# The causal mask of expert attention, moved from a TensorE matmul into the VectorE operation that takes the row maximum

## The chip, the cores and the metric

The kernel runs on one core of a Trainium2 chip, as one launch. The metric is the device time of that core in microseconds (us). A core has TensorE (PE; its weight loads are shown as PEld), VectorE (DVE), ScalarE (ACT), GpSimd (POOL) and SyncE (SP, which issues DMAs). Each works through its own queue in order and waits on semaphores for the others. SBUF and PSUM are the on-chip memories of 128 partitions; matmuls write PSUM.

## The reference

Three stages follow each other: a sparse attention of 8 heads, a mixing stage (rotation by a learned angle, token mixing, channel mixing), and an attention with four experts per batch. Only the last is touched. Cut to what matters:

```python
logits = x @ w_gate                      # x: 4 batches, 576 positions, 512 wide
# w[:, :, e]: softmax over the two largest of the 4 logits, 0 for the others
for e in range(4):
    q = x @ wq[e]; k = x @ wk[e]; v = x @ wv[e]          # 64 wide
    scores = (1 / 8) * (q @ k.transpose(0, 2, 1))         # 576 x 576
    causal = np.triu(np.ones((S, S), dtype=bool), 1)
    scores = np.where(causal, -1000000000.0, scores)
    scores = scores - scores.max(-1, keepdims=True)
    a = np.exp(scores)
    a /= a.sum(-1, keepdims=True) + 1e-09
    out += w[:, :, e:e+1] * (a @ v @ wo[e])
```

## The kernel before

The expert stage runs over 4 batches and 4 experts, and for each of these 16 pairs (function `attention`) over five tiles of queries t = 0 to 4, of 128 rows each and 64 in the last. Tile t scores against the 128(t+1) keys that causality leaves, so 128, 256, 384, 512 and 576; the last goes in two chunks of 288, since a score tile is 512 wide. That makes 80 tiles and 96 chunks. Products are made from a high and a low part of their operands.

Per chunk, PE multiplies q by the keys (line 585) and by their low part (586) into a PSUM tile `s`, of which there are three. In the last chunk of a tile a third matmul (588) adds the causal mask: the table `mask_cr`, 0 on and below the diagonal and a large negative number above it, times an identity `identr`. This matmul covers only the 128 (or 64) columns of the diagonal block. DVE then takes the negated row maximum `nm` from `s` (590; 597 joins the two chunks of tile 4). ACT computes Exp of `s` with `nm` as bias, writes the SBUF tile `p` and collects the row sum `sm` (601). Each such ACT line stands as two instructions in the trace: the Exp, and the read of the accumulator. DVE adds 1e-9 to `sm` and inverts it (605, 606), POOL scales `p` by it and by the gate (608; DVE does it for tile 0), PE transposes `p` into PSUM `tp` (611), ACT copies that to `pthi` (619), DVE makes the low part `ptlo` (620), and the matmuls of lines 563 and 567 multiply with the values. `p` has four buffers, so a tile's `p` can be written once the transposes of the tile four earlier are done.

Between the tiles stand units of other work (`fill`), released after a tile's last score matmul: the projections of the next pair and batch (`pq`, `pv`, with `q`, `k`, `klow`, `lg` made from them by ACT, DVE and POOL), and the output products `po` of the batch before. The functions give the dependencies and a rough sequence; a list scheduler then sets the order of each engine's queue from a simulated timeline. At the stage's start six POOL memsets clear halves of the low key tiles `klow` (449), then `lg` (458), whose zeros DVE overwrites in part (485).

## Time and profile before

| | us |
|---|---|
| median of 3 runs | 572.19 (572.13 to 573.19) |
| profiled execution, span | 571.5 |
| PE busy in it | 534.9 (94%) |
| DVE busy | 409.1 (72%) |
| ACT busy | 320.0 (56%) |
| POOL busy | 230.5 (40%) |

The times are of whole executions; the span is what the profiler recorded of one, and the rows are on its clock. The duration in a row is that of one instruction; where the next one of the same engine starts before it has ended, the distance from start to start is shorter than the duration. The expert stage takes the time from about 374 us to the end; some of its first projections lie before.

### The profile page before, as it was taken

The numbers are of one execution on the slowest core, as the hardware profiler recorded it, in microseconds if no ns is written. First come the engines' busy times: TensorE is split into PE (matmuls) and PEld (weight loads), VectorE is DVE, ScalarE is ACT, GpSimd is POOL, SyncE is SP. The second block draws the span as 40 slices with busy tenths as digits, with TensorE's granted clock in tenths as the row PEclk, the third lists the DMA queues.
The fourth block names the chain that finished last, engine by engine and source line by source line (L and its number), as shares of the span: only waits on it lengthen the run. The fifth ranks groups of instructions, "written<-read, shape, count | busy, mean of one in ns | idle before, by whom it ended". The sixth has DMA issues, their size and how long they took to land.

```text
span 571.5 us, 12545 instructions
## 1 busy us (share of the span) xinstructions
PE 534.9 (94%) x4536; PEld 509.9 (89%) x4536; DVE 409.1 (72%) x1211; ACT 320.0 (56%) x906; POOL 230.5 (40%) x317
## 2 busy tenths in 40 slices
PE   6859698899999999999999999898999999999987
PEld 6748598899999999999999999897989999999987
DVE  3898799757686556766356553588988898888972
ACT  5875976525435326263152450375778767857873
POOL 3453565421156111545104570354454634644451
PEclk9959889999999999999999999998999999999999
DMA  9659443333122004110100020100001101100012
GB/s 291 216 171 307 132 156 96 87 95 124 37 86 86 16 23 133 37 30 1 56 1 1 1 58 0 38 1 2 0 11 43 33 1 32 51 4 12 32 43 84
DMA packets 20390, 37.55 MB, mean 66 GB/s; under 512 B 2904, under 2 KB 10248, under 8 KB 20328
## 3 DMA queue, kind: packets, MB, share of 16 engines
q1 hardware_dynamic: 20328, 36.74, 20.4%
q8 instruction: 36, 0.59, 0.5%
q14 instruction: 26, 0.21, 0.1%
HBM read 32.01 MB, written 4.72 MB: 64 GB/s over the span
## 4 chain that ended last, share of the span: by engine, by line
PE 64%; DVE 17%; ACT 11%; DMA 3%; issue 3%; POOL 2%; SPq 0%; DVEq 0%; POOLq 0%; ACTq 0%
PE y L256 6%; PE y L257 6%; PE y L258 6%; PE s L181 3%; PE th L256 3%; PE th L258 3%; PE th L257 3%; PE tp L611 3%; DVE X L133 2%; PE g L257 2%; PE g L256 2%; PE av L234 2%; PE g L258 2%; DVE nm L590 2%; DMA k<-in_kl 2%
## 5 line engine op out<-in xcount | busy, mean ns | idle before, releaser
L256 PE MATMUL y<-wtk_hi,zhi 128*128 128x288 f32 x288 | 86.5, 301 | 0.5 <-DVE X L339 0.4
L257 PE MATMUL y<-wtk_lo,zhi 128*128 128x288 f32 x288 | 85.9, 299 | 0.0
L258 PE MATMUL y<-wtk_hi,zlo 128*128 128x288 f32 x288 | 84.7, 296 | 0.0
L324 POOL TENSOR_TENSOR zlo<-cs,zhi 128x512 fp32r<-128x512 f32 (+1 forms) x40 | 48.4, 1221 | 66.5 <-DVE zhi L321 45.5
L208 POOL TENSOR_TENSOR p<-p,sm 128x288 f32<-128x288 f32 (+2 forms) x48 | 30.6, 643 | 93.4 <-DVE sm L207 54.0
L608 POOL TENSOR_SCALAR p<-p,sm,gt 128x256 f32<-128x256 f32 (+1 forms) x64 | 45.2, 708 | 52.7 <-DVE sm L606 35.3
L601 ACT ACTIVATE p<-s,nm 128x128 f32<-128x128 f32 (+2 forms) x96 | 49.5, 518 | 14.4 <-DVE nm L590 7.9
L256 PEld LDWEIGHTS y<-wtk_hi,zhi 128*128 128x128 f32 x288 | 54.0, 188 | 1.7 <-DVE X L339 1.1
L252 POOL TENSOR_TENSOR x_lo<-X,x_hi 128x576 fp32r<-128x576 f32 x24 | 35.7, 1491 | 46.9 <-DVE x_hi L250 40.5
L257 PEld LDWEIGHTS y<-wtk_lo,zhi 128*128 128x128 f32 x288 | 54.1, 188 | 0.3
L258 PEld LDWEIGHTS y<-wtk_hi,zlo 128*128 128x128 f32 x288 | 53.9, 188 | 0.1
L256 PE MATMUL th<-wth_hi,x_hi 128*128 128x256 f32 (+1 forms) x160 | 48.4, 303 | 3.3 <-ACT X L241 2.9
L590 DVE TENSOR_REDUCE nm<-s 128x1 f32<-128x128 f32 (+2 forms) x96 | 44.3, 469 | 5.3 <-PE s L588 4.4
L258 PE MATMUL th<-wth_hi,x_lo 128*128 128x256 f32 (+1 forms) x160 | 46.2, 290 | 0.0
L181 PE MATMUL s<-k,q 128*108 128x54 f32 (+2 forms) x320 | 43.8, 282 | 2.5 <-DMA k<-in_kl 2.5
L257 PE MATMUL th<-wth_lo,x_hi 128*128 128x256 f32 (+1 forms) x160 | 46.1, 289 | 0.0
L181 PEld LDWEIGHTS s<-k,q 128*108 128x108 f32 (+1 forms) x320 | 42.0, 203 | 3.8 <-issue 2.3
L215 ACT COPY pt<-tp 96x384 f32<-96x384 f32 (+2 forms) x44 | 20.9, 477 | 36.2 <-PE tp L211 36.0
L256 PE MATMUL pq<-x_hi,wqk_hi 128*128 128x288 f32 x128 | 39.8, 311 | 1.0 <-DVE q L536 0.7
L256 PE MATMUL g<-u_hi,wch_hi 128*128 128x288 f32 x128 | 39.2, 306 | 0.0
L620 DVE TENSOR_TENSOR ptlo<-tp,pthi 128x128 fp32r<-128x128 f32 (+4 forms) x80 | 37.7, 479 | 1.1 <-ACT pthi L619 0.6
L257 PE MATMUL pq<-x_lo,wqk_hi 128*128 128x288 f32 x128 | 38.0, 297 | 0.0
(173 smaller groups left out, 1728.7 us busy)
## 6 DMA issues: line engine op xcount, KB each, us to landing
X<-in_wtk SPq DMA_DIRECT2D x18, 288.0 KB
q<-in_qs SPq DMA_DIRECT2D x8, 594.0 KB
q<-in_ql SPq DMA_DIRECT2D x8, 576.0 KB
v<-in_vl SPq DMA_DIRECT2D x24, 144.0 KB
out_t<-X SPq DMA_DIRECT2D x20, 128.0 KB
k<-in_kl SPq DMA_DIRECT2D x8, 304.0 KB
k<-in_ks SPq DMA_DIRECT2D x8, 288.0 KB
X<-in_wth SPq DMA_DIRECT2D x8, 256.0 KB
```

The lines of the kernel that those rows point to most:

```text
L181: nc.tensor.matmul(s[:rm, i * kw:i * kw + w], qt[:, j0 + i, :], kt[:, k0:k0 + w], start=False, stop=i == n - 1)
L208: nc.gpsimd.tensor_tensor(tiles(p), tiles(p), each(sm), op=ALU.mult)
L215: copy(pt[:kw, :n * rm], tp[:kw, :n * rm])
L252: eng.tensor_tensor(lo, x, f(hi), op=ALU.subtract)
L256: nc.tensor.matmul(ps, ahi, bhi, start=first, stop=False)
L257: nc.tensor.matmul(ps, ahi, blo, start=False, stop=False)
L258: nc.tensor.matmul(ps, alo, bhi, start=False, stop=last)
L324: nc.gpsimd.tensor_tensor(lo, zf, f(hi), op=ALU.subtract)
L590: nc.vector.tensor_reduce(nm[:w, t + ci:t + ci + 1], s[:w, :c1 - c0], axis=AX.X, op=ALU.max, negate=True)
L601: nc.scalar.activation(p[:w, c0:c1], scs[ci][:w, :c1 - c0], AF.Exp, bias=nm[:w, t:t + 1], scale=1.0, accum_out=acc)
L608: eng.tensor_scalar(p[:w, :kn], p[:w, :kn], sm[:w, t:t + 1], gt[:w, t, e:e + 1], op0=ALU.mult, op1=ALU.mult)
L620: nc.vector.tensor_tensor(dst(ptlo), src, f(dst(pthi)), op=ALU.subtract)
```

## The change

The mask matmul goes, and with it the tables `mask_c`, `identr` and `mask_cr`. A table `later` of 128 x 640 (bf16) takes their place: 512 columns of zeros and 128 of the diagonal mask. One DVE operation per chunk (`tensor_tensor_reduce`) adds the right stretch of it to `s`, negates, writes the result to `p`, and takes the minimum into `nm`. Exp then reads `p`, with scale −1, and writes it in place. The PSUM tile `s` is thus free after the DVE operation.

```diff
-    mask_c = new_mask("mask_c", [128, 128], const)
-    select(mask_c, [[-1, 128]], 0, 1, MASKED)
...
-    identr, mask_cr = (cw.tile([128, 128], F32R, name=name) for name in ("identr", "mask_cr"))
-    nc.vector.tensor_copy(identr, ident)
-    nc.vector.tensor_copy(mask_cr, mask_c)
+    later = cw.tile([128, 640], BF16, name="later")
+    nc.gpsimd.memset(later[:, :512], 0.0)
+    nc.gpsimd.memset(later[:, 512:], 0.0)
+    select(later[:, 512:], [[-1, 128]], 0, 1, MASKED)
...
-                nc.tensor.matmul(s[:w, :c1 - c0], q[:, ts], kl[:, c0:c1], start=False, stop=not last)
-                if last:
-                    scored = nc.tensor.matmul(s[:w, t0 - c0:t0 - c0 + w], identr[:, :w], mask_cr[:, :w],
-                                              start=False, stop=True)
-                nc.vector.tensor_reduce(nm[:w, t + ci:t + ci + 1], s[:w, :c1 - c0], axis=AX.X, op=ALU.max,
-                                        negate=True)
+                scored = nc.tensor.matmul(s[:w, :c1 - c0], q[:, ts], kl[:, c0:c1], start=False, stop=True)
+                z0 = 512 - t0 + c0 if c1 == kn else 0
+                nc.vector.tensor_tensor_reduce(p[:w, c0:c1], s[:w, :c1 - c0], later[:w, z0:z0 + c1 - c0], op0=ALU.add,
+                                               op1=ALU.min, scale=-1.0, scalar=3.0e38,
+                                               accum_out=nm[:w, t + ci:t + ci + 1])
...
-                nc.scalar.activation(p[:w, c0:c1], scs[ci][:w, :c1 - c0], AF.Exp, bias=nm[:w, t:t + 1], scale=1.0,
+                nc.scalar.activation(p[:w, c0:c1], p[:w, c0:c1], AF.Exp, bias=nm[:w, t:t + 1], scale=-1.0,
                                      accum_out=acc)
```

The queue of DVE in batch 0 where expert 3 begins and expert 2 ends, before. The names carry the expert, the tile and the chunk (`s_3_1_0`: expert 3, tile 1, first chunk), then a running number; the brackets say on which engines an instruction waits:

```order
L590 TENSOR_REDUCE nm_3_5441<-s_3_1_0_5474 128x1 [waits PE_49]
L620 TENSOR_TENSOR ptlo_2_5260<-tp_2_1_5331,pthi_2_5259 128x2x128 [waits Activation_49]
L605 TENSOR_SCALAR sm_3_5440<-sm_3_5440 128x1 [waits Activation_49]
L509 TENSOR_REDUCE mx_5317<-gt_5100 128x5 [waits DVE_49]
L620 TENSOR_TENSOR ptlo_2_5260<-tp_2_2_5346,pthi_2_5259 128x3x128 [waits Activation_49]
L536 SCALAR_TENSOR_TENSOR q_0_1_5367<-pq_0_0_1_5448,q_0_1_5367 64x288 [waits Activation_49]
L606 RECIPROCAL sm_3_5440<-sm_3_5440 128x1 [waits DVE_49]
L510 TENSOR_SCALAR mx_5317<-mx_5317 128x5 [waits DVE_49]
L605 TENSOR_SCALAR sm_3_5440<-sm_3_5440 128x1 [waits Activation_49]
L590 TENSOR_REDUCE nm_3_5441<-s_3_2_0_5508 128x1 [waits PE_49]
L540 TENSOR_TENSOR klow_0_4666<-pq_0_1_0_5479,k_0_0_5368 64x288 [waits Activation_49]
```

And now; a line called ISA is the fused operation or, with one column and no source, the read of its accumulator:

```order
L615 TENSOR_TENSOR ptlo_2_5247<-tp_2_1_5316,pthi_2_5246 128x2x128 [waits Activation_49]
L600 TENSOR_SCALAR sm_3_5422<-sm_3_5422 128x1 [waits Activation_49]
L506 TENSOR_SCALAR cnt_5287<-cnt_5287 128x20 [waits DVE_49]
L585 ISA p_3_1_5454,nm_3_5423<-s_3_1_0_5455,later 128x256 [waits PE_49,Pool_49]
L585 ISA nm_3_5423 128x1
L615 TENSOR_TENSOR ptlo_2_5247<-tp_2_2_5330,pthi_2_5246 128x3x128 [waits Activation_49]
L601 RECIPROCAL sm_3_5422<-sm_3_5422 128x1 [waits DVE_49]
L507 TENSOR_TENSOR gt_5091<-gt_5091,cnt_5287 128x20 [waits DVE_49,Activation_49]
L535 SCALAR_TENSOR_TENSOR q_0_0_5349<-pq_0_0_1_5429,q_0_0_5349 64x288 [waits Activation_49]
L603 TENSOR_SCALAR p_3_0_5424<-p_3_0_5424,sm_3_5422,gt_4676 128x128 [waits DVE_49]
L508 TENSOR_REDUCE mx_5302<-gt_5091 128x5 [waits DVE_49]
L600 TENSOR_SCALAR sm_3_5422<-sm_3_5422 128x1 [waits Activation_49]
```

The fused operation of tile 1 stands behind the low part of the older expert's tile 1 and not ahead of it, is followed by a second instruction, and waits for POOL as well as PE, since the POOL scale and the transposes of an older tile use the same buffer of `p`.

The queue of ACT at the same place, before:

```order
L601 ACTIVATE p_3_0_5442,sm_3_5440<-s_3_0_0_5443,nm_3_5441 128x128 [waits Pool_49]
L619 CAST pthi_2_5259<-tp_2_2_5346 128x3x128 [waits PE_49]
L535 ACTIVATE q_0_1_5367<-pq_0_0_1_5448 64x288 [waits DVE_49]
L601 ACTIVATE p_3_1_5473,sm_3_5440<-s_3_1_0_5474,nm_3_5441 128x256 [waits DVE_49,Pool_49]
L539 CAST k_0_0_5368<-pq_0_1_0_5479 64x288 [waits PE_49]
L572 COPY tmp_2_0_5357<-o_2_0_5352 64x256 [waits PE_49,Activation_49]
L619 CAST pthi_2_5259<-tp_2_3_5391 128x4x128 [waits PE_49]
```

And now:

```order
L596 ACTIVATE p_3_0_5424,sm_3_5422<-p_3_0_5424,nm_3_5423 128x128 [waits DVE_49]
L614 CAST pthi_2_5246<-tp_2_2_5330 128x3x128 [waits PE_49]
L505 ACTIVATE gt_5091<-lg_5088 128x20 [waits DVE_49]
L534 ACTIVATE q_0_0_5349<-pq_0_0_1_5429 64x288 [waits PE_49]
L596 ACTIVATE p_3_1_5454,sm_3_5422<-p_3_1_5454,nm_3_5423 128x256 [waits DVE_49]
L534 ACTIVATE q_0_1_5350<-pq_0_0_1_5429 64x288 [waits DVE_49]
L538 CAST k_0_0_5351<-pq_0_1_0_5459 64x288 [waits PE_49]
```

The wait for POOL has left the Exp line: it reads and writes the tile that DVE has already written.

The queue of POOL at the start of the expert stage, before:

```order
L102 TENSOR_TENSOR wvg_lo<-wvg_st_4251,wvg_hi 128x260 [waits DMAHW0_49,Activation_49]
L102 TENSOR_TENSOR wvg_lo<-wvg_st_4255,wvg_hi 128x260 [waits DMAHW1_49,Activation_49]
L449 MEMSET klow_0_4662 64x576 [waits PE_49,Pool_49]
L449 MEMSET klow_1_4663 64x576
L449 MEMSET klow_0_4664 64x576
```

And now:

```order
L100 TENSOR_TENSOR wvg_lo<-wvg_st_4250,wvg_hi 128x260 [waits DMAHW1_49,Activation_49]
L442 MEMSET later 128x512 [waits PE_49]
L443 MEMSET later 128x128
L448 MEMSET klow_0_4659 64x576 [waits Pool_49]
L448 MEMSET klow_1_4660 64x576
```

Two memsets of `later` stand ahead of the six of `klow`, behind which `lg` follows in both, and the wait for PE has passed from the first of `klow` to the first of `later`.

## Rows read from the trace of the kernel before

**Rows 1.** Engine windows of the expert stage (columns named in its first line).

```profile
core 0: us, PE busy (x) PEld busy (x) DVE busy (x) ACT busy (x) POOL busy (x), PEclk, DMA share, GB/s
...
496.00:552.00 56.00, 55.92 (x438) 53.96 (x436) 49.09 (x182) 41.10 (x129) 26.03 (x47) 1.00 0.08 28
...
sum 197.50, PE 188.66 PEld 179.01 DVE 163.78 ACT 141.43 POOL 92.57; mean PE 37.73 PEld 35.80 DVE 32.76 ACT 28.29 POOL 18.51
```

**Rows 2.** Chain of waits by line: 374 to 390, 390 to 460, 460 to 496, 496 to 552.

```profile
by line: DVE nm L590 21.8%; DVE x_lo L252 17.4%; DVE q L536 11.4%; ACT wo_hi L100 7.2%; ACT x_hi L248 7.2%; ACT p L601 6.5%; ACT k L539 4.8%; DVE ptlo L620 3.3%; issue 3.1%; DVE sm L605 3.0%; DVE klow L540 2.8%; ACT q L535 2.6%; DVE X L573 
by line: PE tp L611 10.2%; PE s L585 7.6%; PE o L567 6.9%; PE s L586 6.3%; PE pv L258 5.9%; PE o L563 5.5%; PE pv L256 5.2%; PE pv L257 5.1%; PE pq L257 4.8%; DVE nm L590 4.8%; PE pq L256 4.7%; PE pq L258 4.6%; ACT p L601 4.1%; DVE ptlo L62
by line: DVE nm L590 16.2%; DVE q L536 10.3%; ACT p L601 9.8%; DVE ptlo L620 8.8%; issue 8.2%; DVE klow L540 7.1%; DVE X L573 6.2%; DVE x_lo L252 4.4%; ACT x_hi L248 4.0%; DVE p L608 3.5%; DVE sm L606 3.4%; DVE cmp L500 2.9%; DVE sm L605 2.
by line: PE tp L611 12.5%; PE s L585 8.8%; PE pq L256 8.6%; PE o L567 8.2%; PE s L586 8.0%; PE pq L257 7.9%; PE pq L258 7.6%; PE o L563 6.6%; PE po L256 5.2%; PE po L257 4.6%; PE po L258 4.6%; PE pv L256 3.8%; PE pv L258 3.5%; PE pv L257 3.
```

**Rows 3.** Instruction groups by form: busy us, mean ns of one, then idle before.

```profile
L293 ACT ACTIVATE cs<-cs,halfpi 128x256 f32<-128x256 f32 x32 | 15.9, 497 | 0.1
...
L588 PE MATMUL s<-mask_cr,identr 128*128 128x128 f32 x64 | 15.2, 238 | 0.0
...
L590 DVE TENSOR_REDUCE nm<-s 128x1 f32<-128x512 f32 x16 | 10.9, 683 | 0.3 <-PE s L588 0.2
L620 DVE TENSOR_TENSOR ptlo<-tp,pthi 128x512 fp32r<-128x512 f32 x16 | 10.9, 681 | 0.5 <-ACT pthi L619 0.4
...
L601 ACT ACTIVATE p<-s,nm 128x256 f32<-128x256 f32 x16 | 7.6, 475 | 3.9 <-DVE nm L590 3.4 <-POOL p L608 0.2 <-DVE sm L605 0.2
...
L590 DVE TENSOR_REDUCE nm<-s 128x1 f32<-128x128 f32 x16 | 4.6, 285 | 3.0 <-PE s L588 2.9
```

**Rows 4.** Timeline of PE, 445.4 to 446.4: start us, duration us, instruction.

```profile
445.62 0.44 PE L585 MATMUL s<-k,q 128*128 128x512 f32 x1
445.90 0.39 PE L586 MATMUL s<-klow,q 128*128 128x512 f32 x1
446.13 0.22 PE L588 MATMUL s<-mask_cr,identr 128*128 128x128 f32 x1
446.19 0.29 PE L585 MATMUL s<-k,q 128*64 128x288 f32 x1
```

**Rows 5.** Timeline of DVE, 390.5 to 391.5.

```profile
390.77 0.13 DVE L605 TENSOR_SCALAR sm<-sm 128x1 f32<-128x1 f32 x1
390.83 0.47 DVE L620 TENSOR_TENSOR ptlo<-tp,pthi 128x320 fp32r<-128x320 f32 x1
```

**Rows 6.** Timeline of ACT, 427.2 to 427.5.

```profile
427.23 0.19 ACT L601 ACTIVATION_READ_ACCUMULATOR p<-s,nm 64x1 f32 x1
427.32 0.48 ACT L601 ACTIVATE p<-s,nm 64x288 f32<-64x288 f32 x1
```

**Rows 7.** What PE idled for before the first score matmul: us, times.

```profile
  ACT p L601: 2.9, 8
```

**Rows 8.** Timeline of DVE and ACT, around 379.5 and around 552.

```profile
379.27 0.45 DVE L590 TENSOR_REDUCE nm<-s 64x1 f32<-64x288 f32 x1
...
379.74 0.52 ACT L619 CAST pthi<-tp 128x128 fp32r<-128x128 f32 x2
...
551.40 0.44 DVE L590 TENSOR_REDUCE nm<-s 64x1 f32<-64x288 f32 x1
...
553.13 0.27 ACT L619 CAST pthi<-tp 128x128 fp32r<-128x128 f32 x1
```

**Rows 9.** Timelines of POOL, DVE and PE at the stage's start.

```profile
357.10 3.70 POOL L449 MEMSET klow<- 64x576 f32 x6 [14.27 <-PE g L258]
...
360.89 0.16 DVE L485 COPY lg<-pv 128x4 f32<-128x4 f32 x1 [0.80 <-POOL lg L458]
...
361.20 0.36 PE L256 MATMUL pv<-wvg_hi,x_hi 128*128 128x260 f32 x1 [0.53 <-DVE lg L485]
```

## The prediction

> **What bounds the kernel now.** The change touches the expert stage, the last 197.5 us of the span of 571.5, and a few instructions before it. I read four views, widest first. The engine windows over that stage [rows 1] show TensorE (PE) and VectorE (DVE) both near full: 189 and 164 us busy of 197.5, and in the stretch 496–552 PE is busy for 55.92 of 56.00 while DVE is busy for 49.09, which leaves DVE 12% free. So work taken from PE and given to DVE has little room. The chain of waits by line [rows 2] says who sets the pace where. In 390–460 and 496–552 only PE lines stand ahead: PE-run stretches, 126 us. In 374–390 and 460–496 the reduce that is changed leads the chain (21.8 and 16.2%), with other DVE lines behind it: DVE-run stretches, 52 us. The remaining 19.5 us (552–571.5) are the tail. So I weigh a PE saving spread evenly over the stage with 126/197.5 = 0.64 and a DVE cost with 52/197.5 = 0.26.

> Next I read the durations by form [rows 3] and then the start times on PE and DVE [rows 4, 5], because the busy time of one instruction overlaps the next on both engines: what an instruction costs is the distance from its start to the start of the next.

> **Removed: the mask matmuls.** There are 80 (16 batch-expert pairs of 5 tiles), 64 of them 128 columns wide and 16 of them 64 wide. Their rows say 238 ns each [rows 3], which would make some 18 us for the 80; that is not their price. On the timeline [rows 4] the mask matmul starts at 446.13 and the next matmul at 446.19: 0.06 us. The matmul behind it is slower as well: the first score matmul of 512 columns stands right behind a mask matmul and takes 0.28 (445.62 to 445.90), the second of equal size, not behind one, takes 0.23 (445.90 to 446.13). So 0.06 + 0.05 = 0.11 us each, 64 × 0.11 = 7.0; for the 16 narrow ones I take about half, 1.0. Together 8.0 us of PE. If the extra 0.05 stays with whatever comes next, only 64 × 0.06 and half of that for each narrow one, 16 × 0.03, go: 4.3; if the full busy time counted, 18. I take 8.0: the start times are the nearest rows. On the path: 8.0 × 0.64 = −5.1 us.

> **Changed: the row maximum.** 96 reduces of PSUM become 96 fused operations that read the same PSUM scores and a bf16 mask from SBUF and write the negated sum to SBUF beside the minimum. No row of before has this operation. The nearest is the subtraction that also reads PSUM and SBUF and writes SBUF: 681 ns at 512 columns, against 683 for the reduce [rows 3]. So the main part: 0. Lower end: below nothing is excluded, since it reads the same number of elements. Upper end: two passes per element. From 285 ns at 128 to 683 at 512 the reduce pays 1.04 ns per element [rows 3]; a partition sees 16 × (128 + 256 + 384 + 512 + 576) = 29,696 elements, so +31 us of DVE. I take 0 and keep 31 for a rival.

> **Added: an accumulator read per operation.** The program now has a second DVE instruction behind each of the 96, which writes the maximum. Nearest rows: a one-column DVE operation starts at 390.77 and the next at 390.83, 0.06 us [rows 5]; ScalarE's (ACT) own accumulator read takes 0.19 and its successor starts 0.09 after it [rows 6]. Ends: 96 × 0.06 = 5.8 and 96 × 0.19 = 18.2 us of DVE. I take 0.08, between the two start-to-start rows: 7.7 us. In DVE-run stretches 7.7 × 0.26 = +2.0. Elsewhere the PE cover hides it: in 496–552 DVE would go to 49.09 + 2.2 = 51.3 of a stretch that has shrunk to 53.7, still covered, with 4% to spare. If that cover is gone, all 7.7 count.

> **Changed: Exp reads SBUF in place.** Rows: Exp of 128x256 from PSUM 475 ns, an ACT function of the same size with a bias operand from SBUF 497 [rows 3]: +22 ns, 96 × 0.022 = 2.1 us of ACT, which is on the chain for about a tenth (4.1 to 9.8% at the Exp line [rows 2]): +0.2. [...]

> **Moved: the release of buffers.** Two things swap. (a) The three score buffers in PSUM are freed by the DVE operation and no more by Exp. PE waited 2.9 us for Exp in front of the first score matmul [rows 7]; I take −1, since some of it only changes its name. (b) The SBUF tile p (four of them) is now written by DVE about 1.1 us before Exp wrote it, and DVE must wait until the transposes of the tile four earlier are done. In order of tiles, 33 of 76 reduces began before their slot was free. The first: 379.27, while the ACT copy that follows those transposes begins only at 379.74; the last: 551.40 against 553.13 [rows 8]; the longest such lead was 3.3 us and all together make 47. What is queued behind on DVE is the low-part subtraction, the small sums and the gate work, for which ACT, POOL and PE wait. The new order puts the fused operation behind such work of older tiles (the DVE rows shown with the change), so that most of the lead is taken out by order. Ends: 0 and 6 (about an eighth of 47); I take +1.

> **Added: the table `later`.** Two POOL memsets stand before the six of `klow` and take over their wait for PE. The six take 3.70 us for 576 columns each, so 640 columns cost 3.70/6 × 640/576 = 0.7. Behind them waits the chain klow, lg, DVE's copy at 360.89 (0.80 idle), PE at 361.20 (0.53 idle) [rows 9]: all of it late by 0.7, so +0.7, less if POOL starts them earlier. The removed memset, selection and two casts of the old mask stood at the kernel's start and beside other work: 0.

> **Sum.** −5.1 + 2.0 + 0.2 − 1 + 1 + 0.7 = −2.2 us. On the profiled span of 571.5 that is 569.3; the median 572.19 lies 0.7 above that span, so the forecast is 570.0.

> **Rivals.** *No change:* the matmul behind keeps its 0.05, PE gets back 4.3 × 0.64 = 2.8, and the additions of 2.0 + 0.2 + 0.7 (a and b cancelling) eat it: 0.1 net, about 572. For it: the surplus appears on every matmul of another weight behind a narrow one. Against: the second score matmul, now ahead of it, is wide.

> *Slower: DVE becomes the bound.* The accumulator read takes its full 0.19 without overlap (18.2 us) and the fused operation holds DVE's queue for its p slot. Then DVE in 496–552 needs 49.09 + 18.2 × 56/197.5 = 54.3 plus waits, against PE's 53.7: PE's saving no longer shows. It decides from about 0.16 us per read on, or less with waits. Price: no PE gain, 18.2 × 0.26 = 4.7 in the DVE-run stretches, and up to 6 of waits, less the 1 of (a), plus 0.9: 572.2 + 5 to 10, most of it at the lower end; I set 577. For it: DVE has only 12% free and the lead of 47 us. Against: start-to-start distances of small operations on two engines are 0.06 and 0.09.

> *Much slower: half rate.* DVE gets +31 + 7.7; its 164 us become 203 for a stage of 197.5, with some waits around it: near 590. Against it: the subtraction with the same kinds of operands runs at full rate [rows 3]. [...] No run shows the operation itself.

> **Chances and range.** Forecast 46% (its own range 566 to 571), no change 19%, DVE-bound 26%, half rate 9%. From these: faster by over 0.2% (1.14 us, about what a measurement of this kernel can tell) 0.46, within 0.2% 0.19, slower 0.35. The range reaches down to 565, where PE's saving comes through with no DVE cost (−5.1 − 1 − 1), and up to 580, through most of the DVE-bound case; half rate lies outside.

> **What would show it.** Right: the accumulator read starts its successor within 0.1 us; the fused operation of 512 columns takes about 0.68; PE in 496–552 stays at 99% over a shorter stretch; the PE-run windows end some 4 to 5 us earlier in all; the first score matmul of 512 columns takes 0.23. Wrong: a fused operation near 1.1 us; DVE idle with POOL or PE as the releaser before the fused line, for more than 6 us in all; PE idle for DVE in stretches that PE ran before; a start of the stage later by more than 1 us.

## The result, and the profile after

The changed kernel takes 577.72 us (median of 4; 576.99 to 580.66) against 572.27 of the kernel before; the ratio is 1.0097, with a 95% interval of 1.0074 to 1.0119. It is slower, by about 1%. A later job (a session in which runs and the kernel before are measured together) gave 1.0100 (1.0059 to 1.0141). Over all jobs the kernel before has medians of 572.3 to 573.4, so experiments are compared by their ratios to it in the same job, not by single medians.

The windows of the expert stage, on the times of [rows 1] (the columns are those named there):

```profile
496.00:552.00 56.00, 53.48 (x408) 50.30 (x408) 47.59 (x204) 41.86 (x125) 25.07 (x44) 1.00 0.08 28
552.00:575.20 23.20, 18.68 (x113) 16.92 (x112) 7.69 (x29) 8.06 (x26) 4.64 (x8) 0.76 0.16 52
sum 201.20, PE 188.23 PEld 173.44 DVE 163.43 ACT 146.92 POOL 93.19; mean PE 37.65 PEld 34.69 DVE 32.69 ACT 29.38 POOL 18.64
```

DVE is busy no longer than before (163.43 against 163.78), though 96 instructions were added. But PE, which was full in 496–552, is now 2.5 us short of it (over the whole of 374–552 it is busy for 169.6 of 178 us, before for 173.8), and in the tail its granted clock is 0.76 on average. The forms that answer to [rows 3]:

```profile
L585 DVE CUSTOM_DVE_ANT_0 p<-s,later 128x512 f32<-128x512 f32 x16 | 11.0, 685 | 1.2 <-POOL p L603 0.6 <-POOL olo L637 0.5
...
L596 ACT ACTIVATE p<-p,nm 128x256 f32<-128x256 f32 x16 | 8.1, 509 | 0.5 <-DVE nm L585 0.2
...
L585 DVE DVE_READ_ACCUMULATOR2_ANT nm<- 128x1 f32 x64 | 5.2, 82 | 0.0
```

The fused operation is as fast as the reduce was (685 ns against 683), Exp from SBUF is 34 ns slower, and the accumulator read lasts 82 ns. What DVE's own timeline shows of that read (start, duration):

```profile
551.88 0.67 DVE L585 CUSTOM_DVE_ANT_0 p<-s,later 128x512 f32<-128x512 f32 x1
...
552.48 0.08 DVE L585 DVE_READ_ACCUMULATOR2_ANT nm<- 128x1 f32 x1
552.48 0.48 DVE L615 TENSOR_TENSOR ptlo<-tp,pthi 128x320 fp32r<-128x320 f32 x1
```

The next instruction starts with the read. From the fused operation to the next work it is 0.61 us at 512 columns (median of 16), from the reduce it was 0.60: the read is all but free.

The price is in another view: what DVE idled for in front of the fused line, and who waited for that line (us, times):

```profile
its engine sat idle before it (us, times) until:
  PE tp L606: 5.4, 10
...
  PEld s L582: 3.4, 9
  PE s L582: 0.9, 3
```

The reduce never waited for transposes (it waited 4.6 us, for scores alone). Now DVE stands still for 5.4 us until PE has transposed an older tile and so freed a buffer of p. One such place, for the last pair's tile 0, in the timeline of the changed kernel:

```profile
545.92 0.44 PE L606 MATMUL tp<-ident,p 128*128 128x128 f32 x2
...
546.30 0.19 ACT L596 ACTIVATION_READ_ACCUMULATOR p<-p,nm 64x1 f32 x1
...
546.51 0.29 DVE L585 CUSTOM_DVE_ANT_0 p<-s,later 128x128 f32<-128x128 f32 x1 [1.28 <-PE tp L606]
...
547.60 0.16 DVE L601 RECIPROCAL sm<-sm 64x1 f32<-64x1 f32 x1
547.65 0.46 POOL L636 TENSOR_SCALAR ohi<-X 128x320 fp32r<-128x320 f32 x1 [1.48 <-DVE X L572]
```

DVE idles for 1.28 us until the transposes at 545.92 are done. Behind it in its queue stand the sums and the reciprocal of another tile, without which POOL can't scale, and the sum into X, for which POOL idles 1.48 us. POOL's scaled tiles are what PE transposes next, so such a wait can go round and come back to PE. That it does is argued, not shown: behind this place PE works without a pause until 550.9, where it waits 0.46 us for the fused operation of another tile, and its two longest pauses in the stage (1.9 and 1.4 us) are ended by other work. PE's waits in 470–530 (us, times, longest):

```profile
PE s L582 <- POOL k L540: 1.9, 1, 1.9
PE pq L254 <- DVE q L535: 1.4, 1, 1.4
```

How much of these two goes back to waits for p is open.

PE's pauses then meet the clock. Windows around the end (PE's busy time is the second number, the granted clock the third from the end), first the changed kernel, then the kernel before:

```profile
548.00:550.40 2.40, 2.40 (x20) 2.08 (x18) 2.33 (x8) 2.20 (x6) 1.75 (x3) 1.00 0.19 68
550.40:556.80 6.40, 3.99 (x26) 2.72 (x25) 5.20 (x24) 4.38 (x14) 2.11 (x4) 1.00 0.01 4
557.60:567.20 9.60, 9.60 (x48) 8.95 (x47) 2.31 (x6) 3.35 (x10) 2.42 (x5) 0.50 0.12 41
568.00:572.40 4.40, 4.40 (x40) 4.36 (x38) 1.07 (x3) 0.93 (x4) 0.00 (x0) 1.00 0.42 135
```

```profile
552.00:556.80 4.80, 3.36 (x25) 2.66 (x23) 3.49 (x15) 3.64 (x13) 2.07 (x4) 1.00 0.01 2
557.60:567.20 9.60, 9.05 (x76) 8.41 (x74) 3.12 (x8) 3.99 (x12) 2.27 (x4) 1.00 0.30 98
```

In the changed kernel PE was busy for 3.99 of 6.40 us; then its clock was at 0.50 for the 9.6 us in which it makes the last products without a pause. In the same 9.6 us the kernel before got through 76 matmuls at full clock, this one through 48. The kernel before had paused there too, for 1.44 of 4.80 us, and kept its clock: a pause by itself does not tell that the clock falls. In this execution the last tile's `pthi` comes only 0.7 us later than before (558.7 against 558.0), and PE ends 3.7 us later (572.6 against 568.9): here the loss arrives almost wholly in the tail.

### The profile page after: what moved, and what is told of

Read it like the earlier page. It is cut to its first block, busy times and chain, and to the rows that moved or that the text cites. A ratio compares the mean times of both kernels' runs of the same rounds, so it can differ in the third digit from the quotient of the medians.

```text
span 575.2 us, 12470 instructions
## 1 busy us (share of the span) xinstructions
PE 534.0 (93%) x4456; PEld 503.9 (88%) x4456; DVE 408.5 (71%) x1305; ACT 325.1 (57%) x906; POOL 231.3 (40%) x318
## 4 chain that ended last, share of the span: by engine, by line
PE 65%; DVE 16%; ACT 10%; issue 3%; DMA 2%; POOL 2%; SPq 0%; DVEq 0%; POOLq 0%; ACTq 0%
PE y L254 6%; PE y L255 6%; PE y L256 6%; PE s L179 4%; PE tp L606 3%; PE th L254 3%; DVE X L131 3%; PE th L256 3%; PE th L255 3%; PE g L255 2%; PE g L254 2%; PE av L232 2%; PE g L256 2%; PE s L582 2%; DMA k<-in_kl 2%
## 5 line engine op out<-in xcount | busy, mean ns | idle before, releaser
L596 ACT ACTIVATE p<-p,nm 128x128 f32<-128x128 f32 (+2 forms) x96 | 52.9, 552 | 8.8 <-DVE nm L585 6.2
L585 DVE CUSTOM_DVE_ANT_0 p<-s,later 128x128 f32<-128x128 f32 (+2 forms) x96 | 43.8, 472 | 8.8 <-PE tp L606 5.4
L606 PE MATMUL tp<-ident,p 128*128 128x128 f32 (+1 forms) x240 | 37.0, 267 | 1.8 <-POOL p L603 0.7
```

The source lines that it names most:

```text
L585: nc.vector.tensor_tensor_reduce(p[:w, c0:c1], s[:w, :c1 - c0], later[:w, z0:z0 + c1 - c0], op0=ALU.add, op1=ALU.min, scale=-1.0, scalar=3 ...
L596: nc.scalar.activation(p[:w, c0:c1], p[:w, c0:c1], AF.Exp, bias=nm[:w, t:t + 1], scale=-1.0, accum_out=acc)
L606: nc.tensor.transpose(tp[:, c * w:(c + 1) * w], p[:w, 128 * c:128 * c + 128], ident[:w, :w])
```

## The experiments

Two theories: *slot* (VectorE's queue now waits for a buffer of p, and that loses the time) and *clock* (the tail at half clock is the loss, whatever made PE pause). Later a third, *order*: the scheduler chose another order, and that is luck. The scheduler sets the queues anew for every edit. By their traces e5 and e7 have the order of the changed kernel, e12 and e13 that of e6, e8 that of e3, and e14 that of the kernel before; e3, e4, e6, e9 to e11 and e15 to e18 each have an order of their own. Medians in us, ratio to the kernel before in the same job with its interval, DVE's idle for transposes in front of the fused line:

| run | kernel | median | ratio | idle |
|---|---|---|---|---|
| – | changed, 4 buffers of p | 577.72 | 1.0097 (1.0074–1.0119) | 5.4 |
| e5 | the same again | 579.55 | 1.0100 (1.0059–1.0141) | 5.6 |
| e7 | 4 buffers; tmp, cnt, cmp cut | 577.70 | 1.0089 (1.0056–1.0122) | 5.4 |
| e18 | 4 buffers, other order | 578.16 | 1.0088 (1.0058–1.0118) | 4.3 |
| e10 | 3 buffers | 595.34 | 1.0391 (1.0368–1.0415) | 18.2 |
| e6 | 5 buffers; tmp, cnt, cmp cut | 572.79 | 0.9993 (0.9973–1.0012) | 2.4 |
| e13 | 5 buffers; q cut | 573.04 | 0.9992 (0.9972–1.0013) | 3.3 |
| e12 | 5 buffers, dummy matmuls | 573.32 | 1.0006 (0.9991–1.0021) | 2.6 |
| e3 | sum to PSUM, 4 buffers | 572.58 | 0.9981 (0.9959–1.0004) | none |
| e11 | sum to PSUM, 3 buffers | 572.65 | 0.9987 (0.9969–1.0004) | none |
| e8 | sum to PSUM, 80 fused | 574.29 | 1.0027 (1.0006–1.0049) | none |
| e1 | changed, dummy matmuls at the end | 575.97 | 1.0048 (1.0031–1.0064) | 5.5 |
| e2 | changed, last pair in old form | 576.18 | 1.0036 (1.0016–1.0056) | |
| e4 | before without mask matmul | 571.84 | 0.9975 (0.9958–0.9991) | |
| e9 | before, 5 buffers | 576.50 | 1.0044 (1.0026–1.0061) | |
| e14 | before, q cut | 573.11 | 0.9992 (0.9969–1.0016) | |
| e15 | before with copies into p | 576.13 | 1.0051 (1.0027–1.0075) | 1.0 |
| e16 | before with copies into nm | 582.33 | 1.0150 (1.0111–1.0188) | |
| e17 | before with free copies | 582.29 | 1.0158 (1.0130–1.0185) | |

**The end of the kernel.** e1, e2:

```diff
# e1: the changed kernel, last pair
+            for _ in range(2 if ending else 0):
+                nc.tensor.matmul(tp[:w, :512], q[:, ts], k[:, :512], start=True, stop=True)
             for c in range(t + 1):
                 nc.tensor.transpose(...)
# e2: old form (mask matmul, reduce, Exp from s) where (b, e) == (B - 1, NE - 1)
```

> The changed kernel with two dummy score matmuls of 512 columns ahead of each tile's transposes in the last batch-expert pair alone; their result is overwritten. They add 10 x 0.23 = 2.3 us to PE where nothing hides them and keep PE busy where it paused (550 to 557). Theory 'clock' (the loss is that PE's pauses there are followed by ten microseconds at half the granted clock, while PE runs the last products): granted clock in the tail stays at 1.00 or falls for a much shorter time, and the time falls from 577.7 to 572 to 575, although work was added. Theory 'VectorE' (the added VectorE work and the waits for a slot of p cost the time everywhere, the clock is beside the point): no gain, 577.5 to 580.

> The changed kernel, but the last of the 16 batch-expert pairs in the old form (mask matmul, reduce, Exp from PSUM). 'Clock': the last pair runs as before, PE does not pause for longer than it did, the clock in the tail stays up, 571 to 573. 'VectorE': a sixteenth of the loss comes back, 0.3 us, so 577 to 578.

e1 is faster than the changed kernel by 2.8 us (the difference of the ratios) with 2.3 us of work added; 2.7 us of the loss stay. Both runs came out between the theories; 2 of e2's 12 executions are at 572 to 573. In e1's profile the tail is at full clock, but three earlier stretches of 3.4 us are at half, together as long as the one of the first profile (mean clock 0.967 in both). The fair pair is e1's profile and e5's below: the same three stretches in both, the tail at half clock in e5 alone, mean clocks of 0.967 and 0.958, and spans of 575.7 and 578.1 us. So the half-clock tail did cost. The clock carries a part; that it is not the root is for the next runs to show.

**The slot taken away.** In e3 the sum goes back to PSUM, and ScalarE alone waits for p, as before:

```diff
-                nc.vector.tensor_tensor_reduce(p[:w, c0:c1], s[:w, :c1 - c0], ...
+                nc.vector.tensor_tensor_reduce(s[:w, :c1 - c0], s[:w, :c1 - c0], ...
...
-                nc.scalar.activation(p[:w, c0:c1], p[:w, c0:c1], AF.Exp, ...
+                nc.scalar.activation(p[:w, c0:c1], scs[ci][:w, :c1 - c0], AF.Exp, ...
```

> The changed kernel, but the fused operation writes its sum back into the PSUM score tile and Exp reads it there and writes p. The wait for a slot of p leaves VectorE's queue (5.4 us of idle before the fused line in the changed kernel), Exp reads PSUM again (32 ns less each, 3 us of ScalarE), and the score buffers are held until Exp as before; the 96 accumulator reads stay. 'VectorE' with the slots as the cause: 2 to 4 us faster than the changed kernel, 573.5 to 575.5. 'VectorE' with the accumulator reads as the cause: no change, 577 to 578. 'Clock': as the tail's pauses go, either way; the clock column decides.

All of the loss goes, more than was expected. In front of e3's fused line DVE waits only for the scores (us, times):

```profile
  PE s L584: 3.8, 8
```

e5, e6 and e7 differ in buffer counts alone:

```diff
-            p = cp.tile([128, 640], F32, tag="p", bufs=4, ...)
+            p = cp.tile([128, 640], F32, tag="p", bufs=5, ...)        # e6
-            tmp = cp.tile([64, S - 256], F32, tag="tmp", ...)         # two buffers
+            tmp = cp.tile([64, S - 256], F32, tag="tmp", bufs=1, ...) # e6, e7; cnt, cmp alike
```

> The changed kernel unaltered, to have it in the same job as the three beside it and to see a second profile. If the time of 577.7 is its own: 576.5 to 578.5. If stretches at half the granted clock fall by chance and the first runs had many of them: down to 575. In the earlier runs of these kernels every execution had 27 to 34 us at half clock before the expert stage and 3.4, 6.8 or 10.2 in it, so the profile should again show a multiple of 3.4.

> The changed kernel with five buffers of p and not four; to make room the tiles tmp, cnt and cmp have one buffer and not two. VectorE still writes p, Exp still reads it from SBUF. If the wait for a slot of p is what costs (theory 'slots'): VectorE's idle before the fused line on transposes falls from 5.4 us to under 2, and the time to 573 to 575, near the variant that writes its sum to PSUM (572.6). If Exp's reading from SBUF or VectorE's writing to SBUF costs (theory 'SBUF'): no gain against the four-buffer control, 576 to 578.

> Control for the run with five buffers: four buffers of p as in the changed kernel, and tmp, cnt and cmp with one buffer. Both theories: as the changed kernel or up to 1 us slower, 577 to 579.

The fifth buffer removes the loss, the control keeps it. It does not remove all of the wait (under 2 us was expected), and e5's median lies 1 us above what was expected of it. The idle in front of e6's fused line:

```profile
  PE tp L606: 2.4, 6
```

e5's profile has the half clock not in one place but in four. Two of them with what came ahead of each:

```profile
420.00:424.40 4.40, 3.85 (x23) 2.61 (x24) 4.24 (x16) 3.48 (x12) 2.25 (x5) 0.98 0.01 2
424.60:427.60 3.00, 3.00 (x16) 2.91 (x15) 1.27 (x10) 1.61 (x6) 0.82 (x2) 0.50 0.13 44
492.00:496.40 4.40, 2.48 (x17) 2.14 (x17) 4.14 (x10) 4.33 (x11) 3.80 (x4) 0.95 0.08 27
496.60:499.60 3.00, 3.00 (x15) 2.29 (x15) 2.63 (x9) 1.16 (x4) 1.33 (x3) 0.54 0.00 0
```

Each time PE had paused (0.5 and 1.9 us of 4.4). In the first profile of the same kernel, in the same order, PE had paused as long in 420–424.4 (busy for 3.84 us), and its clock stayed full until 557. By such windows e5 spends 20 us of the stage at half clock, the first profile of the same kernel 10, that of the kernel before 3.4; e5's span is 2.9 us longer than the first profile's (578.1 against 575.2).

**The slot made worse.** e10 is the changed kernel and e11 is e3, both with

```diff
-            p = cp.tile([128, 640], F32, tag="p", bufs=4, ...)
+            p = cp.tile([128, 640], F32, tag="p", bufs=3, ...)
```

> The changed kernel with three buffers of p and not four: the suspected wait made worse. 'Slot in VectorE's queue': VectorE's idle before the fused line on transposes grows from 5.5 us to over 15, PE pauses more, more stretches at half clock, 585 to 605. If the slots were not the cause: within 2 us of 578.

> The variant that writes its sum back to PSUM, with three buffers of p: here the slot is waited for by ScalarE's Exp and not by VectorE, as in the kernel before. 'Slot in VectorE's queue': three buffers hurt, but less than in the changed kernel with three, by at least a third: 575 to 590 and below that run. Rival 'the slot matters wherever it is waited for': the same loss as there.

e10's idle in front of the fused line:

```profile
  PE tp L606: 18.2, 16
```

The third buffer less costs about 17 us (0.0294 × 573, against the changed kernel) where VectorE waits, and nothing where ScalarE does, though 575 to 590 was expected there. This is the sharpest pair: same buffers, same operation, another queue that waits. Two more things differ: the order, and that Exp reads SBUF in e10 and PSUM in e11; but e6 reads SBUF too and loses nothing.

**Order, and what the loss hid.** e9 and e14 are the kernel before with e6's and e13's buffer counts; e13 has `bufs=5` on p and on q (before: 4 and 6); e12 is e6 with e1's dummy matmul once per tile and not twice. e18 is the changed kernel, and e8 is e3, with

```diff
+                if c1 < kn:                                # first chunk of tile 4
+                    nc.vector.tensor_reduce(nm[:w, t + ci:t + ci + 1], s[:w, :c1 - c0], ..., negate=True)
+                    continue                               # its Exp reads s with scale 1.0
```

> The kernel before with five buffers of p (tmp, cnt and cmp at one buffer, as in the run of the changed kernel with five). It is the control for that run: a fifth buffer may help any kernel. Theory 'slot in VectorE's queue' (the change made a slot of p needed before VectorE may go on, and that alone lost the time): the kernel before does not wait for slots there, so no gain, 572.3 to 574. Rival 'more buffers help anyway': it gains as the changed kernel did, 4 to 5 us, to 568.

> The changed kernel with five buffers of p, and room made for the fifth by one buffer of q less (five, not six) while tmp, cnt and cmp keep two. In the run with five buffers before, tmp had one, and the same cut made the kernel before 3 us slower, so the change's own gain may have been hidden. 'Slot in VectorE's queue': with the slot gone and tmp back, PE's 4.4 us of removed work shows at last, 568 to 572, below the kernel before. If the sixth q or the rest of the change eats it: 572 to 575.

> Control for the run beside it: the kernel before with five buffers of q, nothing else changed. No theory speaks against it: 572.5 to 574; where it is slower, the run beside it is to be read against this.

> The changed kernel with five buffers of p and one dummy matmul of 512 columns ahead of each tile's transposes in the last batch-expert pair (5 x 0.23 = 1.2 us of work that counts for nothing). With five buffers one stretch of 3.4 us at half clock remained at 554 to 558, where PE sets the pace: worth up to 1.7 us. 'Clock': it goes or moves to where PE waits anyway, and the time falls by 0.5 to 1.5 us below 572.8, or at least does not rise. If the clock is not what carries the loss: 573.5 to 574.

> The changed kernel with four buffers of p, in which the 16 first chunks of tile 4, which need no mask, keep the plain reduce and Exp from PSUM. It keeps the slot wait in VectorE's queue for all 80 tiles, but the scheduler gives PE and VectorE another order (the four-buffer control e7 had the very order of the changed kernel, so that the loss with four buffers has been seen in one order alone). 'Slot in VectorE's queue': 575.5 to 578.5 again. Rival 'order': as the runs without the slot, 572 to 574.

> The variant that writes its sum back to PSUM, and in which the 16 first chunks of tile 4, which need no mask, keep the plain reduce: 80 fused operations and accumulator reads and not 96. If an accumulator read costs about its 0.08 us on a VectorE that sets the pace a quarter to a half of the time, 16 fewer are worth 0.3 to 0.6 us: 572.0 to 572.4 against 572.6, which is hardly to be told apart. A gain of over 1.5 us would say that the reads cost more than their rows show.

A fifth buffer does not help the kernel before (with tmp cut it is 2.5 us slower, where up to 1 us was expected), so e6's gain is no general gift of memory. e18 answers *order*: it has the wait in an order of its own and loses the same 0.9%. The gain with five buffers is seen in one order alone. e13 shows that the forecast gain does not come once the wait is smaller; it ties. e12 says nothing of the clock: the mean of its profiled execution is 0.966 beside e6's 0.970, and the time stayed (a ratio of 1.0006 beside 0.9993). e8 missed: by the ratios it is 2.6 us slower than e3 in place of 0.2 to 0.6 faster, in the same order. On record beside each time is the mean granted clock of the whole execution: 8 of e8's 12 executions have 0.967 or less and a median of 575.1 us, the other 4 have 572.7; of e3's 12 only 2 are as low. So this loss goes with the clock; why e8's falls more often is open.

**PE's half alone.** From the kernel before:

```diff
-                last = ci == len(chunks) - 1
...
-                nc.tensor.matmul(s[:w, :c1 - c0], q[:, ts], kl[:, c0:c1], start=False, stop=not last)
-                if last:
-                    scored = nc.tensor.matmul(s[:w, t0 - c0:t0 - c0 + w], identr[:, :w], mask_cr[:, :w],
-                                              start=False, stop=True)
+                scored = nc.tensor.matmul(s[:w, :c1 - c0], q[:, ts], kl[:, c0:c1], start=False, stop=True)
```

> The kernel before without the mask matmul and with nothing in its place: the mask is left out, everything else as before. This is the PE half of the change alone. By the prediction's term 5.1 us faster than before (567), by the bare start-to-start distance of 0.06 us 2.8 us faster (569.5). If it is not faster than 571, the PE half never was worth the forecast, and VectorE's cost is small.

1.4 us (0.5 to 2.4): half of the lower of the two values that the expectation gives, and not faster than 571. So the PE half never was worth the forecast; that VectorE's cost is then small did not come true with the wait. Without it, it did: e3, the change without the wait, Exp from SBUF and the early release of the score buffers, has a ratio of 0.9981 beside e4's 0.9975. The 1.4 us hold a new order as well.

**Is the wait enough by itself?** One line behind the reduce of the kernel before, for each tile's first chunk:

```diff
+                if ci == 0:
+                    nc.vector.tensor_copy(p[:w, 0:1], s[:w, 0:1])      # e15
+                    nc.vector.tensor_copy(nm[:w, 7:8], s[:w, 0:1])     # e16 in its place
+                    nc.vector.tensor_copy(junk[:w, 0:1], s[:w, 0:1])   # e17 in its place
```

> The kernel before with one thing added: behind the reduce of each tile's first chunk VectorE copies one column of the score tile into column 0 of p, which Exp then overwrites. VectorE thus needs the slot of p before it goes on, as in the changed kernel, and PE's mask matmul, the reduce and Exp from PSUM all stay. 80 copies of one column. 'Slot in VectorE's queue': slower than the kernel before by 4 to 8 us, and than the control beside it by 3 to 7. If the loss needs something else of the change: as the control.

> Control for the run with the added slot wait: the same 80 one-column copies, into an unused column of nm and not into p, so that VectorE has the same work and waits for no slot. Both theories: 80 x 0.06 to 0.13 us more VectorE work, 573 to 576.

> A second control for the run with the added slot wait: the same 80 one-column copies, now into a small tile of their own with eight buffers that nobody reads, since the control before wrote into nm, which Exp reads, and came out slower than the run it was to control. 'Slot in VectorE's queue': 573 to 574.5, below the 576.1 of the run with the slot wait. Rival 'order' (any change of VectorE's queue gives the scheduler another order, and that moves the time by several microseconds either way): anywhere from 573 to 582, with no regard to slots.

This failed as a test. Both controls, without a slot wait, are slower than e15, and e15 idles for only 1.0 us for transposes. So it isn't shown that the wait alone slows the kernel before. Nor do the runs price a DVE microsecond: the same 80 copies, 0.147 us each (median in e15; from start to start [rows 5] have 0.06 for a one-column operation, so 4.8 us of DVE by estimate), cost 2.9 us in e15, 8.6 in e16 and 9.1 in e17 (0.0051, 0.0150 and 0.0158 × 573). e17's expectation allowed *order* 573 to 582 and the slot 573 to 574.5; 582.29 speaks for *order* or for the added work, and no run parts the two. So a new order may move this kernel by more than the whole loss. What speaks for the wait all the same is that the loss follows it through the variants of the changed kernel: 0.9 to 1.0% in two orders with four buffers, 3.9% with three, and none in the orders of e3, e6 and e11 (in e3's, e8 loses 0.3%).

## Why the prediction was wrong

The step that failed is the release of p, "(b)" of the part on buffers: "The new order puts the fused operation behind such work of older tiles [...] so that most of the lead is taken out by order", priced at +1 of a range from 0 to 6. The mechanism was named, with the queue and what stands behind it; its size was wrong. DVE's idle for slots is 5.4 us after scheduling, of 47 us of lead, and its price is 6.6 us by e3 (0.0116 × 573) and 5.5 by e6 beside its control e7 (0.0096 × 573), so about the upper end of 6 and not 1. Taking the wait away (e3) or to under half (e6) brings back the whole 0.9 to 1.0%; making it longer by 13 us (e10 against the changed kernel) costs about 17. The forecast of 2.2 us faster missed the 5.5 us slower (0.0097 × 572) by 7.7: this term is 4.5 to 5.6 of it, the mask matmuls are 3.7 (e4), and the reads, which cost next to nothing, take 2 off again.

The deeper error is the weighting. I read the chain's shares as prices: a PE microsecond 0.64, a DVE microsecond 0.26. The runs give PE 1.4/8.0 or 1.4/4.3, so 0.2 to 0.3 (e4), and for DVE's idle 6.6/5.4 = 1.2 (e3) or 16.8/12.8 = 1.3 (e10), each with a new order in it; for DVE's work they give no one price (0.6 to 1.9 for the same copies, by the estimate of 4.8 us). That PE stands in the chain means that it was the last to finish, not that time taken from it comes back in full: DVE at 88% busy ran right behind it. Why the factor of DVE's idle is above one I can only argue, and no run shows it: its delay makes PE pause, and what follows at half clock is longer again (in 9.6 us of the tail 48 matmuls at 0.50, where there had been 76 at 1.00).

Point by point. *Mask matmuls* (−5.1): mis-sized, −1.4 in e4. The start distances were right, the weight of 0.64 was not; the score matmul of 512 columns that had 0.28 in [rows 4] now takes 0.24:

```profile
442.66 0.40 PE L582 MATMUL s<-k,q 128*128 128x512 f32 x1
442.90 0.39 PE L583 MATMUL s<-klow,q 128*128 128x512 f32 x1
443.13 0.30 PE L582 MATMUL s<-k,q 128*64 128x288 f32 x1
```

*Fused operation* (0): right, 685 ns at 512 columns where the reduce took 683; half rate is out. *Accumulator reads* (+2.0): wrong to the good side, 0.01 each in place of 0.08. *Exp from SBUF* (+0.2): 34 ns at 256 columns (509 against 475) where the rows of before gave 22. *PSUM release* (−1): wrong, the wait changed its name and grew: PE and its weight loads wait 4.3 us (12 times) for the fused operation, where it was 2.9 (8) for Exp [rows 7]. *The table* (+0.7): about right, by two memsets ahead of `klow`; PE's matmul of 361.20 [rows 9] starts 0.5 us later, at 361.72:

```profile
356.95 0.53 POOL L442 MEMSET later<- 128x512 bf16 x1 [14.31 <-PE g L256]
357.42 0.20 POOL L443 MEMSET later<- 128x128 bf16 x1
357.68 3.64 POOL L448 MEMSET klow<- 64x576 f32 x6
```

Of the rivals, the DVE-bound one had the sign and the time (577), and its waits for slots; but its main price, reads of 0.19 us, was not there, and its place was wrong: DVE is no busier, it stands still. That its time came right is luck. The sign that was to speak against the forecast, DVE idle for PE or POOL before the fused line for over 6 us, was there: 7.8 us, 5.4 of it for transposes (before the reduce it was 4.6, all for scores).

Open is how much of the 0.9% comes through the clock. e1 gives 2.8 us with up to 2.3 of added work. e10's profile has as much half clock as e5's, 20 us (a mean of 0.98 in 374–552, of 0.82 behind it), and is 18.4 us longer (596.5 against 578.1), so what three buffers add is not the clock. The mean clocks on record say more. 22 of the 120 executions of the kernel before in the experiments' jobs have 0.961 to 0.967 and a median of 575.7 us; the 96 above have 572.8. Of the changed kernel's ten, four are in that range, with a median of 576.4, and six below it, at 578.1 to 581.5. So at a like clock little of the loss is left, and most of it goes with a clock that falls more often, which may be the way in which the wait costs time; no run shows that step. But the 11 executions of e6 and e13 in that range have a median of 572.7: where the clock falls counts too, and these means don't show it. Open are also the way from DVE's waits to PE's pauses, the part of *order*, and why e15 beats its controls. No version beats both kernels beyond doubt; e3 and e11 come nearest, at 0.998 and 0.999 with intervals that just hold 1.

## What to carry to other kernels

When an operation that only read begins to write, it takes over the wait for the buffer it writes, and everything queued behind it on its engine waits too (here 5.4 us of idle with four buffers, 18.2 with three): count the buffers for the longer life, or write where the data already is. A chain of waits says who came last, not what a microsecond on another engine is worth (here its shares gave DVE 0.26, the runs 1.2 to 1.3 for its idle). Small dummy work on one engine measures that price only if the order of the queues stays: here the same copies cost 2.9 or 9.1 us. Look at whether the granted clock falls after a pause before taking a wait for its own length (here 9.6 us at 0.50 came behind 2.4 us of pause).
